# Last two value products of a granule side by side in two PSUM banks, and VectorE's squares and copies behind its partial sums

## Chip, cores, metric

The kernel runs on one core of a Trainium2 chip. The metric is the device time of one execution in microseconds (us), and the spread between runs is told with it.

## The reference

Local attention with 8 global keys, followed by a two-layer network with a squared relu:

```python
# q, k, v: (4, 8, 768, 64); window of 96 keys, 8 global keys
scores = q @ k.T / 8 + bias(slope of the head, distance);  masked outside window and globals
a = softmax(scores)
x = (a @ v).transpose(0, 2, 1, 3).reshape(3072, 512)
h = x @ w_in                       # 512 -> 2048
g = s * relu(h) ** 2 + b
return g @ w_out                   # 2048 -> 512
```

## The kernel before

The 3072 rows are worked off in 12 granules of 256 rows; three granules make one batch entry. Granule j passes through attention while TensorE also computes the first layer of granule j-1 (called m in the code) and the second layer of granule j-2 (called l). The program gives each engine its instructions in the order of its lines, so this order decides who waits. Names used below:

- S: scores of two head pairs into two score banks, then exp on ScalarE; S_mul: the mask multiply on VectorE.
- A(j, hp): value product of head pair hp, hp = 0 to 3. A_norm: reciprocal and multiply on VectorE, which writes xn.
- XT_dma: two DMA transposes xn -> xT, issued on SyncE's queue.
- P1(m, f), in steady granules r(f): eighth f of the first layer, 8 matmuls of 256 columns into a "psh" bank (there are two); relu on ScalarE empties it. Q(m, f) or "act": the square of that eighth, on VectorE or ScalarE.
- W_mm(l, n): one of seven products of a Strassen-like second layer, 8 matmuls each; W_post(l, n): its partial sum on VectorE. Granules 0 to 2 use the plain second layer P2 instead.
- KO and VO: copies of the key and value rings for the next granule.

The value product, which takes its bank by tag:

```python
def A(j, hp, tag="av", norm=True):
    av = PS[tag].tile([P, GB, 2, 65], F32, name="ps_av", tag=tag)   # "av": one bank, "psh": two
    ...  # 8 matmuls (6 in the first granule of a batch entry), 65 columns each
    if norm:
        A_norm(j, hp)
```

A steady granule (5 to 11; granules 3 and 4 are written by another function, `period`):

```python
S((0, 1))
if j > 5:
    Q(m - 1, 7)
W_mm(l, 1)
if j + 2 < NJ:
    pace(j)               # GpSimd waits for xT[j-1], then
    load_granule(j + 2)   # issues the loads of granule j+2
r(0)                      # first use of xT[j-1] = xT[m]
S_mul(j, 0)
W_post(l, 1)
W_mm(l, 2)                # uses a score bank: waits for the exp of S(0)
...
r(2)
W_sw(l, 2)
A(j, 1, norm=False)
A_norm(j, 1)
S((2, 3))
...
r(3)
W_mm(l, 6)
W_post(l, 6)
S_mul(j, 2)
r(4)
Q(m, 3)
S_mul(j, 3)
W_mm(l, 7)
A(j, 2, norm=False)
A_norm(j, 2)
W_post(l, 7)
Q(m, 4)
r(5)
A(j, 3, norm=False)
A_norm(j, 3)
XT_dma(j)
W_mm(l, 5)
W_sw(l, 4)
KO(j + 1); XB(j + 2)      # XB: DMA transposes of k and q
W_post(l, 5)
Q(m, 5)
r(6)
W_mm(l, 4)
VO(j + 1)
W_post(l, 4)
Q(m, 6)
W_mm(l, 3)
W_post(l, 3)              # reads the second score bank and so frees it
W_store(l)
r(7)
W_sw(m, 3)
```

The softmax here doesn't subtract the row's maximum and nothing guards it: scores larger than these inputs give would overflow.

Of the kernel before, what the change touches and what calls it, by code (L numbers as in the profile page):

```python
# [18 lines left out]
def kernel(  # L19
# [407 lines left out]
    def A(j, hp, tag="av", norm=True):  # L427
        b, g = bg(j)
        first = g == 0
        pt = pts.pop((j, hp))  # L430
        if j not in xn:
            xn[j] = xpool.tile([P, GB, H, D], BF16, name="xn", tag="xn", bufs=2)
        av = PS[tag].tile([P, GB, 2, 65], F32, name="ps_av", tag=tag)
        for i in range(GB):
            for hi in range(2):
                h = 2 * hp + hi
                if first:
                    ops = [(i, vaug[b % 2][:, i, h, 0:65])]
                    if i == 1:
                        ops.append((2, vaug[b % 2][:, 0, h, 0:65]))  # L440
                else:
                    ops = [
                        ((0, 3)[i], vaug[b % 2][:, g * GB + i, h, 0:65]),
                        ((1, 2)[i], vos[j][:, i, h, 0:65]),
                    ]
                for n_, (c, vv) in enumerate(ops):
                    nc.tensor.matmul(  # L447
                        av[:, i, hi, :],
                        lhsT=pt[:, hi, c * P : (c + 1) * P],
                        rhs=vv,  # L450
                        start=n_ == 0,
                        stop=n_ == len(ops) - 1,
                    )
        avs[j, hp] = av
        if norm:
            A_norm(j, hp)
            flush()
# [64 lines left out]
    def P1(j, fp, sq="dve"):  # L522
        if j not in gT:
            gT[j] = gpool.tile([P, FC, GT], BF16, name="gT", tag="gT")
        ps = ps_h.tile([P, 2, GT], F32, name="ps_1", tag="psh")
        for i in range(2):
            fc = 2 * fp + i
            for kc in range(KC):
                nc.tensor.matmul(  # L529
                    ps[:, i, :],  # L530
                    lhsT=w_in_bf[:, kc, fc * P : (fc + 1) * P],
                    rhs=xT[j][:, kc, :],
                    start=(kc == 0),
                    stop=(kc == KC - 1),
                )
        gs = gT[j][:, 2 * fp : 2 * fp + 2, :]
        flush()
        if j < W0:
            nc.scalar.activation(gs, ps[:], ACT.Relu)  # L539
        else:  # L540
            nc.scalar.activation(  # L541
                gs.rearrange("p f (r t) -> p f r t", r=2),
                ps[:].rearrange("p f (t r) -> p f r t", r=2),
                ACT.Relu,
            )
        if sq == "act":
            nc.scalar.activation(gs, gs, ACT.Square)  # L547
        elif sq == "late":
            late_sq[j, fp] = gs
        else:  # L550
            pend.append(gs)
# [3 lines left out]
    def Q(j, fp):  # L555
        gs = late_sq.pop((j, fp))
        nc.vector.tensor_tensor(gs, gs, gs, ALU.mult)  # L557
# [97 lines left out]
    def W_sw(j, n):  # L655
        t = gpool.tile([P, HF, P], BF16, name=f"sw{n}", tag=f"sw{n}", bufs=1)
        sw[j, n] = t[:]
        i0, i1, op = {
            1: lambda: (g_blk(j, 1, 0), g_blk(j, 1, 1), ALU.add),
            2: lambda: (sw[j, 1], g_blk(j, 0, 0), ALU.subtract),  # L660
            3: lambda: (g_blk(j, 0, 0), g_blk(j, 1, 0), ALU.subtract),
            4: lambda: (g_blk(j, 0, 1), sw[j, 2], ALU.subtract),
        }[n]()
        nc.vector.tensor_tensor(t[:], i0, i1, op)

    def W_mm(j, n):
        flush()
        if n == 1:
            wt[j, "a"] = ps_o.tile([P, DM], F32, name="ps_w", tag="pso")[:, 0:HC]
        elif n == 2:  # L670
            wt[j, "c"] = ps_a.tile([P, 2, DM], F32, name="ps_wa", tag="scA")[:, 0, 0:HC]
        elif n == 5:
            wt[j, "b"] = ps_b.tile([P, 2, DM], F32, name="ps_wb", tag="scB")[:, 0, 0:HC]
        elif n == 0:
            wt[j, "d"] = ps_a.tile([P, 2, DM], F32, name="ps_wd", tag="scA")[:, 0, 0:HC]
        ps, lhs, rhs, first = {
            1: lambda: ("a", g_blk(j, 0, 0), w_blk(0, 0), True),
            2: lambda: ("c", g_blk(j, 0, 1), w_blk(1, 0), True),
            6: lambda: ("a", sw[j, 2], tw[:, 1], False),
            7: lambda: ("a", sw[j, 3], tw[:, 2], False),  # L680
            5: lambda: ("b", sw[j, 1], tw[:, 0], True),
            4: lambda: ("a", g_blk(j, 1, 1), tw[:, 3], False),
            3: lambda: ("b", sw[j, 4], w_blk(1, 1), False),
            0: lambda: ("d", sw[j, 4], w_blk(1, 1), True),
        }[n]()
        for f in range(HF):
            nc.tensor.matmul(  # L687
                wt[j, ps],
                lhsT=lhs[:, f, :],
                rhs=rhs[:, f, :],  # L690
                start=first and f == 0,
                stop=f == HF - 1,
                skip_group_check=True,
            )
# [229 lines left out]
    def period(j, items, at, late=None, mid=()):  # L924
        SS(j, (0, 1))
        if j + 2 < NJ:
            pace(j)
            load_granule(j + 2)
        run(items, at[0])
        A(j, 0)  # L930
        run(items, at[1])
        A(j, 1)
        for x in mid:
            W_tw(*x)
        SS(j, (2, 3))
        run(items, at[2])
        A(j, 2)
        KO(j + 1)
        run(items, at[3])
        A(j, 3)  # L940
        if late is None:
            XT_dma(j)
        if j + 1 < NJ:
            VO(j + 1)
        if j + 2 < NJ:
            XB(j + 2)
        if late is not None:
            run(items, 1)
            late()
            XT_pe(j, "act", "psh")  # L950
        run(items, 100)
# [1 line left out]
    P2b(0)  # L953
    P2b(1)
    for f in range(4):
        P1(2, f, "act")
    period(
        3,
        [
# [6 lines left out]
            (P2, 2, 0),  # L966
            (P2, 2, 1),
            (P2, 2, 2),
            (P2_bias, 0, 0),
            (P2, 2, 3),  # L970
            (P2_bias, 0, 1),
        ],
        (3, 1, 3, 1),
# [11 lines left out]
    def steady(j):  # L985
        m, l = j - 1, j - 2
        r = lambda f: P1(m, f, "late")

        def S(hps):
            for hp in hps:  # L990
                S_mm(j, hp)
            for hp in hps:
                S_post(j, hp, mul=False)
# [5 lines that stand above are left out]
        if j + 2 < NJ:  # L999
            pace(j)  # L1000
            load_granule(j + 2)
        r(0)
        S_mul(j, 0)
        W_post(l, 1)
        W_mm(l, 2)
        W_sw(l, 1)
        S_mul(j, 1)
        r(1)
        A(j, 0, norm=False)
        W_post(l, 2)  # L1010
        A_norm(j, 0)
        r(2)
        W_sw(l, 2)
        A(j, 1, norm=False)
        A_norm(j, 1)
        S((2, 3))
        Q(m, 0)
        Q(m, 1)
        for f, *a in more(j):
            f(*a)  # L1020
        Q(m, 2)
        r(3)
        W_mm(l, 6)
        W_post(l, 6)
        S_mul(j, 2)
        r(4)
        Q(m, 3)
        S_mul(j, 3)
        W_mm(l, 7)
        A(j, 2, norm=False)  # L1030
        A_norm(j, 2)
        W_post(l, 7)
        Q(m, 4)
        r(5)
        A(j, 3, norm=False)
        A_norm(j, 3)
        XT_dma(j)
        W_mm(l, 5)
        W_sw(l, 4)
        if j + 1 < NJ:  # L1040
            KO(j + 1)
        if j + 2 < NJ:
            XB(j + 2)
        W_post(l, 5)
        Q(m, 5)
        r(6)
        W_mm(l, 4)
        if j + 1 < NJ:
            VO(j + 1)
        W_post(l, 4)  # L1050
        Q(m, 6)
        W_mm(l, 3)
        W_post(l, 3)
        W_store(l)
        r(7)
        W_sw(m, 3)

    for j in range(4, NJ):
        m, l = j - 1, j - 2
        if l < W0:  # L1060
            items = [(P1, m, 0, "act"), (P2, l, 4), (P1, m, 1), (W_tw, 2, 0, 4)]
            items += [(P2, l, 5), (P1, m, 2, "act"), (P2, l, 6), (P1, m, 3), (P1, m, 4, "act")]
            items += [(P2, l, 7), (P1, m, 5, "act"), (P1, m, 6, "act"), (W_tw, 4, 0, 4), (P1, m, 7), (W_sw, m, 3), (W_tw, 4, 4, 8)]
            items[-5:-5] = more(j)
            period(j, items, (4, 2, 2, 1), mid=((2, 4, 8),))
        else:
            steady(j)
    l, m = NJ - 2, NJ - 1
# [74 lines left out]
```

## Time and profile before

| | before |
|---|---|
| time, median of 3 runs | 213.97 us (213.65 to 214.09) |
| span of the profiled run | 211.3 us |
| TensorE busy | 96% |
| VectorE busy | 79% |
| ScalarE busy | 57% |
| granted TensorE clock | 1.00 |

The head of the page of the kernel before (busy us, share of the span, number of instructions):

```profile
span 211.3 us, 5585 instructions
PE 202.4 (96%) x2284; PEld 159.2 (75%) x2293; DVE 166.8 (79%) x400; ACT 120.8 (57%) x185; POOL 71.1 (34%) x98
```

TensorE is what the kernel is short of, but the share alone doesn't say what is left to win. The Trainium skill says so too (page "Perfetto Trace Analysis", section "Identifying the Most-Contended Engine": matmul busy time is no good measure of the distance to the limit). What helps is to read starts: a group of 8 matmuls of 256 columns takes 0.87 us from its start to the start of what follows when nothing waits. A start that comes later is a hole. (A group told with fewer matmuls than it has lacks a record, and a hole just there isn't real.)

The place of the hole, in granules 5 and 6. The timeline of TensorE before (start, duration, engine, line, operation, count; in brackets the idle time and its releaser):

```profile
79.32 1.05 PE L687 MATMUL ps_w<-w_out_bf,gT 128*128 128x256 bf16 x8
80.90 1.03 PE L529 MATMUL ps<-xT,w_in_bf 128*128 128x256 bf16 x8 [0.53 <-DMA xT<-xn]
81.77 1.04 PE L687 MATMUL ps_wa<-w_out_bf,gT 128*128 128x256 bf16 x8
...
95.37 1.05 PE L687 MATMUL ps_w<-w_out_bf,gT 128*128 128x256 bf16 x8
96.30 1.03 PE L529 MATMUL ps<-xT,w_in_bf 128*128 128x256 bf16 x8
97.17 1.04 PE L687 MATMUL ps_wa<-w_out_bf,gT 128*128 128x256 bf16 x8
```

In granule 5 the first W product starts at 79.32 and P1 could follow at 80.19; it starts at 80.90, a hole of 0.7 us, and waits for transposed x. In granule 6 the same place has 0.93 us, so hardly a hole. Granule 10 has one of 0.4 us (157.24 to 158.52).

The last two value products of granule 4, in the same view:

```profile
72.09 1.04 PE L529 MATMUL ps<-xT,w_in_bf 128*128 128x256 bf16 x8
73.47 0.20 PE L447 MATMUL ps_av<-vaug,pt 128*128 128x65 bf16 x1 [0.35 <-DVE pt L419]
...
73.73 1.03 PE L529 MATMUL ps<-xT,w_in_bf 128*128 128x256 bf16 x8
74.94 0.20 PE L447 MATMUL ps_av<-vaug,pt 128*128 128x65 bf16 x1 [0.17 <-DVE xn L465]
```

The third waits for the mask multiply (72.96 to 73.47), the fourth for the norm of the third, because both have the one "av" bank (74.60 to 74.94). And the scores of granule 7:

```profile
110.35 0.28 PE L396 MATMUL ps_s<-qT,ko 64*128 64x128 bf16 x4
110.64 0.29 PE L396 MATMUL ps_s<-qT,kT 64*128 64x128 bf16 x4
```

Four score matmuls take 0.11 to 0.12 us; the step of 0.29 us is a hole of 0.18 us, where the second score bank was still being read by the partial sum W_post(l, 3).

The waits for the weight loads of value products and of P1 (total us, times, longest), before:

```profile
PEld L447 <- DVE xn L465: 2.5, 6, 0.7
PEld L529 <- issue: 2.2, 5, 0.8
PEld L447 <- DVE pt L419: 1.3, 3, 0.6
```

### The profile page before, as it was taken

The page shows a single profiled execution, that of the slowest core. Times are in us where ns is not written, and L with a number is a line of the kernel's source. Part 1 is how long each engine was busy: PE and PEld are TensorE (multiplying, and loading weights), DVE is VectorE, ACT ScalarE, POOL GpSimd, SP SyncE. Part 2 cuts the span into 40 slices and gives each one's busy share as a digit, 9 for nine tenths or more (in the row PEclk, how much of TensorE's full clock was granted, in tenths as well). Part 3 has the DMA queues.
Part 4 walks back from the last instruction along what each step waited for, and adds up shares of the span by engine and source line. Part 5 has one row for each costly group of instructions (what it writes and reads, how often), then busy time and mean ns, then how long its engine had stood idle before and what let it go on. Part 6 is the DMA issues. An engine that isn't in the chain of part 4 may idle for free.

```text
span 211.3 us, 5585 instructions
## 1 busy us (share of the span) xinstructions
PE 202.4 (96%) x2284; PEld 159.2 (75%) x2293; DVE 166.8 (79%) x400; ACT 120.8 (57%) x185; POOL 71.1 (34%) x98
## 2 busy tenths in 40 slices
PE   7989999999999998999999999999999999999992
PEld 2556977456666677887888888888878888888882
DVE  3575658599689698987898898888898899887683
ACT  5559899445997767626536636636445546524400
POOL 8994664930181906407307209109000000000000
PEclk9999999999999999999999999999999999999999
DMA  6999999999499997998999979989965031040022
GB/s 166 192 185 195 187 201 189 180 133 152 75 96 133 235 116 105 172 177 119 145 164 113 204 83 118 200 107 107 210 86 145 36 98 54 0 149 3 0 102 99
DMA packets 103849, 27.63 MB, mean 131 GB/s; under 512 B 91408, under 2 KB 101904, under 8 KB 103824
## 3 DMA queue, kind: packets, MB, share of 16 engines
q0 software_dynamic: 70976, 13.11, 83.1%
q1 hardware_dynamic: 31792, 13.64, 31.8%
q10 hardware_dynamic: 1056, 0.52, 0.9%
q8 instruction: 18, 0.29, 0.6%
q14 instruction: 7, 0.06, 0.1%
HBM read 27.26 MB, written 6.29 MB: 159 GB/s over the span
## 4 chain that ended last, share of the span: by engine, by line
PE 79%; ACT 8%; DMA 5%; DVE 4%; issue 2%; SPq 1%; ACTq 0%
PE ps L529 34%; PE ps_w L687 14%; PE ps_wb L687 6%; PE ps L590 6%; PE ps_av L447 5%; PE ps_s L396 5%; PE ps_wa L687 4%; DMA xT<-xn 3%; ACT pt L409 3%; ACT gT L539 2%; DMA raw<-in_k_dram 2%; DVE xn L465 2%; PE ps_2s L590 2%; PE ps_s L380 1%; ACT gT L547 1%
## 5 line engine op out<-in xcount | busy, mean ns | idle before, releaser
L529 PE MATMUL ps<-xT,w_in_bf 128*128 128x256 bf16 x768 | 97.0, 273 | 1.1 <-DMA xT<-xn 0.8
L529 PEld LDWEIGHTS <-w_in_bf 128*128 128x128 bf16 x768 | 72.5, 98 | 12.9 <-issue 2.2
L541 ACT ACTIVATE gT<-ps 128x512 bf16<-128x512 f32 x72 | 43.0, 597 | 60.1 <-PE ps L529 58.5
L409 ACT ACTIVATE pt<-ps_s 128x1024 bf16<-128x1024 f32 (+1 forms) x48 | 43.1, 952 | 3.0 <-PE ps_s L396 2.9
L419 DVE TENSOR_TENSOR pt<-pt,tmpl 128x1024 bf16<-128x1024 bf16 (+1 forms) x40 | 25.8, 647 | 7.3 <-ACT pt L409 7.0
L687 PEld LDWEIGHTS <-sw 128*128 128x128 bf16 x288 | 27.7, 98 | 3.2
L557 DVE TENSOR_TENSOR gT<-gT 128x512 bf16<-128x512 bf16 x64 | 25.6, 416 | 3.2 <-ACT gT L541 3.1
L112 POOL DMA_DIRECT2D vaug<-in_v_dram x24 | 21.6, 919 | 3.8 <-DMA w_out_bf<-in_moe_w_out_dram 1.8
L687 PEld LDWEIGHTS <-gT 128*128 128x128 bf16 x216 | 20.6, 98 | 3.0
L465 DVE TENSOR_TENSOR xn<-ps_av,rc 128x256 bf16<-128x256 f32 x48 | 20.4, 424 | 1.9 <-DVE rc L464 0.3
L447 PEld LDWEIGHTS <-pt 128*128 128x128 bf16 x352 | 14.9, 98 | 7.5 <-DVE xn L465 2.5
L590 PE MATMUL ps<-w_out_bf,gT 128*128 128x512 bf16 x74 | 18.8, 379 | 0.5 <-issue 0.3
L447 PE MATMUL ps_av<-vaug,pt 128*128 128x65 bf16 x224 | 17.5, 194 | 1.6 <-DVE rc L464 0.6
L687 PE MATMUL ps_w<-tw,sw 128*128 128x256 bf16 x144 | 18.7, 273 | 0.0
L697 DVE SCALAR_TENSOR_TENSOR u<-ps_w,s_bc,bvec 128x256 f32<-128x256 f32 x27 | 12.9, 479 | 6.1 <-PE ps_w L687 6.1
L104 POOL DMA_DIRECT2D qnat<-in_q_dram x18 | 16.0, 904 | 3.2 <-DMA w_out_bf<-in_moe_w_out_dram 1.8
L104 POOL DMA_DIRECT2D knat<-in_k_dram x18 | 15.8, 887 | 3.1 <-issue 2.7
L539 ACT ACTIVATE gT<-ps 128x512 bf16<-128x512 f32 x24 | 14.2, 597 | 4.4 <-PE ps L529 4.3
L126 POOL COPY pdum<-xT 1x1 bf16<-1x1 bf16 x5 | 0.9, 187 | 45.1 <-DMA xT<-xn 45.1
L464 DVE RECIPROCAL rc<-ps_av 128x4 f32<-128x4 f32 x48 | 8.6, 179 | 8.5 <-PE ps_av L447 8.4
L590 PEld LDWEIGHTS <-gT 128*128 128x128 bf16 x96 | 8.6, 98 | 8.2
L396 PE MATMUL ps_s<-qT,kT 64*128 64x128 bf16 x224 | 12.7, 219 | 0.3
(94 smaller groups left out, 241.6 us busy)
## 6 DMA issues: line engine op xcount, KB each, us to landing
out_dram<-o_pr SPq DMA_DIRECT2D x8, 512.0 KB, 4.2
vaug<-in_v_dram POOLq DMA_DIRECT2D x24, 128.0 KB, 7.3
knat<-in_k_dram POOLq DMA_DIRECT2D x22, 128.0 KB, 5.0
qnat<-in_q_dram POOLq DMA_DIRECT2D x22, 128.0 KB, 6.5
w_in_bf<-in_moe_w_in_dram POOLq DMA_DIRECT2D x8, 256.0 KB, 8.3
w_out_bf<-in_moe_w_out_dram POOLq DMA_DIRECT2D x4, 512.0 KB, 9.9
out_dram<-o_pr SPq DMA_DIRECT2D x7, 256.0 KB, 4.0
raw<-in_q_dram ACTq DMA_DIRECT2D x2, 256.0 KB, 4.8
```

What stands on the lines that cost most here:

```text
L104: nc.gpsimd.dma_start(t[:, i, :, :], src[b, :, sb * P : (sb + 1) * P, :].rearrange("h p d -> p h d"))
L112: nc.gpsimd.dma_start(vaug[b % 2][:, sb, :, 0:D], v[b, :, sb * P : (sb + 1) * P, :].rearrange("h p d -> p h d"),)
L396: nc.tensor.matmul(ps[:, hi, oc * P : (oc + 1) * P], lhsT=kt[r, :], rhs=qT[j][r, hp, i * P : (i + 1) * P], start=not biased, stop=not bias ...
L409: nc.scalar.activation(pt[:, :, 0:n], ps[:, :, 0:n], ACT.Exp, scale=QSCALE)
L419: nc.vector.tensor_tensor(pt[:, :, 0:n], pt[:, :, 0:n], m, ALU.mult)
L447: nc.tensor.matmul(av[:, i, hi, :], lhsT=pt[:, hi, c * P : (c + 1) * P], rhs=vv, start=n_ == 0, stop=n_ == len(ops) - 1,)
L465: nc.vector.tensor_tensor(xn[j][:, :, 2 * hp : 2 * hp + 2, :], av[:, :, :, 0:D], rc[:].to_broadcast((P, GB, 2, D)), ALU.mult,)
L529: nc.tensor.matmul(ps[:, i, :], lhsT=w_in_bf[:, kc, fc * P : (fc + 1) * P], rhs=xT[j][:, kc, :], start=(kc == 0), stop=(kc == KC - 1),)
L541: nc.scalar.activation(gs.rearrange("p f (r t) -> p f r t", r=2), ps[:].rearrange("p f (t r) -> p f r t", r=2), ACT.Relu,)
L557: nc.vector.tensor_tensor(gs, gs, gs, ALU.mult)
L590: nc.tensor.matmul(po[j, tb], lhsT=gT[j][:, fc, tb * P : (tb + 1) * P], rhs=w_out_bf[:, fc, :], start=(fc == 0), stop=(fc == FC - 1),)
L687: nc.tensor.matmul(wt[j, ps], lhsT=lhs[:, f, :], rhs=rhs[:, f, :], start=first and f == 0, stop=f == HF - 1, skip_group_check=True,)
```

## The change

The fourth value product moves in front of r(5), next to the third, and takes a "psh" bank; so xn is complete one P1 sooner and x is transposed sooner. The second value product takes a "psh" bank too. VectorE does the partial sums first, then the ring copies and squares. In granule 5 the first P1 goes behind the second W product. In granules 3 and 4 some squares change engine and the order is adapted. The core of the diff:

```diff
     # period (granules 3 and 4)
-        A(j, 1)
+        A(j, 1, "psh")
...
-        A(j, 3)
+        A(j, 3, "psh")
...
-        P1(2, f, "act")
+        P1(2, f, "act" if f % 2 else "late")
+    Q(2, 0)
+    Q(2, 2)
...
     # granule 4
-            period(j, items, (4, 2, 2, 1), mid=((2, 4, 8),))
+            period(j, items, (4, 2, 3, 0), mid=((2, 4, 8),))
...  # P1(3, 3) squared on ScalarE, P1(3, 6) on VectorE
     # steady granules
-        r(0)
+        if j > 5:
+            r(0)
         S_mul(j, 0)
         W_post(l, 1)
         W_mm(l, 2)
+        if j == 5:
+            r(0)
...
-        A(j, 1, norm=False)
+        A(j, 1, "psh", norm=False)
...
         r(4)
-        Q(m, 3)
         S_mul(j, 3)
         W_mm(l, 7)
         A(j, 2, norm=False)
+        A(j, 3, "psh", norm=False)
         A_norm(j, 2)
-        W_post(l, 7)
-        Q(m, 4)
-        r(5)
-        A(j, 3, norm=False)
         A_norm(j, 3)
         XT_dma(j)
+        W_post(l, 7)
+        r(5)
         W_mm(l, 5)
         W_sw(l, 4)
+        W_post(l, 5)
         KO(j + 1); XB(j + 2)
-        W_post(l, 5)
-        Q(m, 5)
         r(6)
+        Q(m, 3)
+        Q(m, 4)
         W_mm(l, 4)
+        W_post(l, 4)
         VO(j + 1)
-        W_post(l, 4)
-        Q(m, 6)
         W_mm(l, 3)
         W_post(l, 3)
         W_store(l)
+        Q(m, 5)
+        Q(m, 6)
```

More of the change, by code (lines that the diff above doesn't have):

```diff
@@ L968 @@
             (P2, 2, 2),
+            (P2, 2, 3),
             (P2_bias, 0, 0),
-            (P2, 2, 3),
             (P2_bias, 0, 1),
@@ L1061 @@
             items = [(P1, m, 0, "act"), (P2, l, 4), (P1, m, 1), (W_tw, 2, 0, 4)]
-            items += [(P2, l, 5), (P1, m, 2, "act"), (P2, l, 6), (P1, m, 3), (P1, m, 4, "act")]
-            items += [(P2, l, 7), (P1, m, 5, "act"), (P1, m, 6, "act"), (W_tw, 4, 0, 4), (P1, m, 7), (W_sw, m, 3), (W_tw, 4, 4, 8)]
+            items += [(P2, l, 5), (P1, m, 2, "act"), (P2, l, 6), (P1, m, 3, "act"), (P1, m, 4, "act")]
+            items += [(P2, l, 7), (P1, m, 5, "act"), (P1, m, 6), (W_tw, 4, 0, 4), (P1, m, 7), (W_sw, m, 3), (flush,), (W_tw, 4, 4, 8)]
             items[-5:-5] = more(j)
-            period(j, items, (4, 2, 2, 1), mid=((2, 4, 8),))
+            period(j, items, (4, 2, 3, 0), mid=((2, 4, 8),))
         else:
```

## The prediction

> **What bounds the kernel now.** TensorE. In the profile's first part it is busy 96% of the 211.3 us span, at a granted clock of 1.00, and the chain of waits that ended last is 79% TensorE. The Trainium skill (page "Perfetto Trace Analysis", section "Identifying the Most-Contended Engine") warns that matmul busy time overstates how near TensorE is to its limit, so I read start-to-start times. In the timeline a group of 8 matmuls (256 columns) starts 0.87 us after the one before, all through the steady granules 6 to 11: one such period takes 15.4 to 15.7 us, of which 8 first-layer and 7 second-layer groups are 15 x 0.87 = 13.1, scores about 1.0, value products about 1.0. Almost nothing is to be won there.
>
> **What can be won: holes in TensorE's timeline (start of the next group less 0.87 us after the last).**
> - Granule 10: first P1 waits for transposed x: 158.11 to 158.52, 0.4 us.
> - Granule 5: the same, 80.19 to 80.90, 0.7 us.
> - Granule 4: third value product waits for the mask multiply (72.96 to 73.47, 0.5 us), fourth for the norm of the third, sharing its bank (74.60 to 74.94, 0.3 us).
> - Granule 3 with P1(2): ScalarE does relu (0.58) plus square (0.63) for each 0.87 us of matmul from 49.4 to 55.2: about 0.2 us at the fourth P1, 0.2 at A(3,1), 0.1 at P2(2,4).
> Sum 2.4 us.
>
> **What the change does.** No operation is added or removed; squares change engine: two of P1(2) go from ScalarE (0.63) to VectorE (0.42), one of P1(3) each way. The fourth value product goes before r(5), so xn is ready about 0.7 us earlier (one P1 of 0.87, less the norm of 0.6 that must queue on VectorE); the transposing DMA takes 4.5 to 5.2 us from issue to first use, so the 0.4 us of granule 10 should go. For granule 5 the first P1 is put behind W_mm 2, which fills the 0.7 us hole, less a possible 0.1 to 0.3 wait for the exp that frees that bank. In granule 4 P1(4) moves before A2: the 0.5 wait goes, A3 then waits about 0.2 for the second mask multiply. In granule 3, less ScalarE work removes about 0.3.
>
> Gain about 1.7 us. Costs: the second value product now takes a turn of the two P1 banks, so P1 r(3) waits for the relu of r(2): that ends at 116.40, r(3) starts at 116.52, so 0 to 0.1 us per period. VectorE, 89% busy in steady periods, gets the same work in another order; delayed squares (5, 6, 7) may come just late for W_mm 2 once or twice. I take 0.3 us off.
>
> **Prediction:** 213.97 - 1.4 = 212.5 us; 8 in 10: 211.1 to 213.9. Faster by over 2%: 0.02; within 2%: 0.97; slower: 0.01.
>
> **What would show it.** The wait of P1 for transposed x (0.8 us in TensorE's wait view) vanishes; the xT transposes are issued about 0.7 us earlier after the fourth value product; the wait of value products for xn (2.5 us, weight-load view) falls by 0.3 to 0.8; ScalarE busy falls by about 1.3 us, VectorE rises by 0.8; from 50 to 81 us the schedule shortens by about 1.3 us; each steady period stays at 15.4 to 15.7 us.
>
> **What would make it wrong.** New TensorE waits each steady period: r(3) on relu, A3 on the second mask multiply (within 0.1 us of the need), or W_mm 2 on late squares: 0.2 us in each of seven periods would eat the gain. Or the earlier transposes land no sooner.

## The result

| | before | after |
|---|---|---|
| time, median of 4 runs | 214.01 us (213.65 to 214.09) | 211.87 us (211.07 to 211.90) |
| ratio | | 0.989 (95%: 0.987 to 0.992) |
| span of the profiled run | 211.3 us | 209.3 us |

So 2.1 us, 1%: clear of noise, and under the 2% that would count as faster. A ratio here is the mean time of one kernel's fast runs over that of the other's in the same rounds, so it isn't quite the ratio of the medians quoted. The head of the page after:

```profile
span 209.3 us, 5603 instructions
PE 201.1 (96%) x2293; PEld 160.8 (77%) x2293; DVE 167.0 (80%) x402; ACT 119.6 (57%) x183; POOL 74.5 (36%) x98
```

Shares tell nothing here. Granules 5 and 6 in TensorE's timeline after:

```profile
78.20 1.05 PE L687 MATMUL ps_w<-w_out_bf,gT 128*128 128x256 bf16 x8
79.31 1.03 PE L687 MATMUL ps_wa<-w_out_bf,gT 128*128 128x256 bf16 x8
80.18 1.91 PE L529 MATMUL ps<-xT,w_in_bf 128*128 128x256 bf16 x16
...
93.71 1.05 PE L687 MATMUL ps_w<-w_out_bf,gT 128*128 128x256 bf16 x8
95.78 1.03 PE L529 MATMUL ps<-xT,w_in_bf 128*128 128x256 bf16 x8 [1.02 <-DMA xT<-xn]
96.65 1.04 PE L687 MATMUL ps_wa<-w_out_bf,gT 128*128 128x256 bf16 x8
```

In granule 5 the hole of 0.7 us is down to 0.24 us (79.31 instead of 79.07). But in granule 6 there is a new one: P1 could start at 94.58 and starts at 95.78, 1.2 us later, waiting for the transposed x of granule 5. That x was issued sooner, as meant. SyncE's queue before and after (start of issue first):

```profile
91.46 3.49 SPq L508 DMA_TRANSPOSE xT<-xn  x2
```

```profile
89.11 3.41 SPq L508 DMA_TRANSPOSE xT<-xn  x2
```

It was issued 2.35 us sooner and was in use 0.52 us sooner (P1 at 95.78 instead of 96.30). The time from issue to landing of its two transposes, each counted from its own issue, in the view of this tile, before and after:

```profile
DMA to landing us min/median/max: 3.5/3.9/4.3
```

```profile
DMA to landing us min/median/max: 5.3/5.7/6.0
```

From the first issue to the last landing the pair took 4.70 us before and 6.54 after. Where one number is given for a pair below, it is counted in this way.

The last value products of granule 4 and the scores of granule 7 after (the other lines of the third and fourth product left out):

```profile
71.51 1.91 PE L529 MATMUL ps<-xT,w_in_bf 128*128 128x256 bf16 x16
73.26 0.19 PE L447 MATMUL ps_av<-vaug,pt 128*128 128x65 bf16 x1
...
73.81 0.20 PE L447 MATMUL ps_av<-vaug,pt 128*128 128x65 bf16 x1
...
109.61 0.28 PE L396 MATMUL ps_s<-qT,ko 64*128 64x128 bf16 x4
109.72 0.28 PE L396 MATMUL ps_s<-qT,kT 64*128 64x128 bf16 x4
```

The third product no longer waits. The fourth follows the third in 0.55 us where 0.25 would do, since the second mask multiply is just late. The hole in the scores of granule 7 is gone. The weight-load waits after:

```profile
PEld L529 <- DMA xT<-xn: 1.3, 1, 1.3
PEld L447 <- DVE xn L465: 1.0, 2, 0.7
PEld L447 <- DVE pt L419: 0.6, 2, 0.3
```

**A ledger of the lead.** The start of a granule's scores marks its place on TensorE. I count it from the first weight load of P1(2,0), where the edited part begins; in front of that the program is the same, but it takes 49.1 to 49.7 us in the profiles, and that alone would blur the reading. Numbers worked out from starts in the traces:

| us from P1(2,0) to | before | after | lead |
|---|---|---|---|
| scores of granule 3 | 4.04 | 3.80 | 0.24 |
| granule 4 | 15.90 | 15.38 | 0.52 |
| granule 5 | 29.57 | 28.44 | 1.13 |
| granule 6 | 45.73 | 44.06 | 1.67 |
| granule 7 | 61.03 | 60.28 | 0.75 |
| granule 8 | 76.69 | 75.67 | 1.02 |
| granule 9 | 92.29 | 91.07 | 1.22 |
| granule 10 | 107.29 | 106.11 | 1.18 |
| granule 11 | 123.35 | 121.56 | 1.79 |
| end | 162.10 | 160.10 | 2.00 |

The lead grows to 1.67 us by granule 6, falls by 0.92 us there, and grows again. Two questions remain: what each part of the change is worth, and why the transposed x of granule 5 lands so late after its issue.

### The profile page after: what moved, and what is told of

The parts are those of the page before. It is cut to its first block, busy times and chain, and to the rows that moved or that the text cites. A ratio compares the mean times of both kernels' runs of the same rounds, so it can differ in the third digit from the quotient of the medians.

```text
span 209.3 us, 5603 instructions
## 1 busy us (share of the span) xinstructions
PE 201.1 (96%) x2293; PEld 160.8 (77%) x2293; DVE 167.0 (80%) x402; ACT 119.6 (57%) x183; POOL 74.5 (36%) x98
## 4 chain that ended last, share of the span: by engine, by line
PE 77%; ACT 10%; DVE 5%; DMA 4%; issue 2%; SPq 0%; ACTq 0%
PE ps L529 34%; PE ps_w L687 14%; PE ps_wb L687 6%; PE ps L590 5%; PE ps_av L447 4%; PE ps_s L396 4%; PE ps_wa L687 4%; ACT pt L409 3%; ACT gT L539 3%; DMA xT<-xn 3%; DMA raw<-in_k_dram 2%; PE ps_2s L590 2%; PE ps_s L380 1%; DVE xn L465 1%; ACT gT L547 1%
## 5 line engine op out<-in xcount | busy, mean ns | idle before, releaser
L419 DVE TENSOR_TENSOR pt<-pt,tmpl 128x1024 bf16<-128x1024 bf16 (+1 forms) x40 | 25.2, 647 | 3.4 <-ACT pt L409 2.9
L557 DVE TENSOR_TENSOR gT<-gT 128x512 bf16<-128x512 bf16 x66 | 25.1, 415 | 1.8 <-ACT gT L541 1.6
L590 PE MATMUL ps<-w_out_bf,gT 128*128 128x512 bf16 x80 | 19.7, 379 | 0.0
L126 POOL COPY pdum<-xT 1x1 bf16<-1x1 bf16 x5 | 4.5, 898 | 42.0 <-DMA xT<-xn 42.0
L447 PEld LDWEIGHTS <-pt 128*128 128x128 bf16 x352 | 15.4, 98 | 3.9 <-DVE xn L465 1.0
L447 PE MATMUL ps_av<-vaug,pt 128*128 128x65 bf16 x224 | 16.4, 193 | 1.0 <-DVE rc L464 0.6
```

The lines of the kernel that those rows point to most:

```text
L419: nc.vector.tensor_tensor(pt[:, :, 0:n], pt[:, :, 0:n], m, ALU.mult)
L447: nc.tensor.matmul(av[:, i, hi, :], lhsT=pt[:, hi, c * P : (c + 1) * P], rhs=vv, start=n_ == 0, stop=n_ == len(ops) - 1,)
L557: nc.vector.tensor_tensor(gs, gs, gs, ALU.mult)
L590: nc.tensor.matmul(po[j, tb], lhsT=gT[j][:, fc, tb * P : (tb + 1) * P], rhs=w_out_bf[:, fc, :], start=(fc == 0), stop=(fc == FC - 1),)
```

## The experiments

Each row of runs that was timed is given with its ratio to the kernel before of the same rounds.

### Parts of the change alone

**r0_only.** The kernel before, with one edit:

```diff
-        r(0)
+        if j > 5:
+            r(0)
...
         W_mm(l, 2)
+        if j == 5:
+            r(0)
```

> The kernel before, with one thing of the change: in granule 5 the first P1 is put behind the second W product. Theory A (leads add up): the 0.7 us hole in front of P1 is filled, less about 0.25 us wait for the bank of the second W product, so 213.5 us, 0.5 less than before. Theory B (an xT landing is tied to the other DMA traffic, not only to its issue): the granule 6 hole in front of P1 opens by up to 0.5 us instead, and the total is 213.8 to 214.0.

Measured: 213.42 us, ratio 0.9991 (0.9975 to 1.0007): no difference shown. Neither theory foresaw the reason. TensorE's timeline of granule 5:

```profile
79.36 1.05 PE L687 MATMUL ps_w<-w_out_bf,gT 128*128 128x256 bf16 x8
...
81.02 1.03 PE L687 MATMUL ps_wa<-w_out_bf,gT 128*128 128x256 bf16 x8 [0.62 <-ACT pt L409]
```

The hole of 0.7 us stayed at the same place (0.79 us) and only changed its name: the second W product needs a score bank, and ScalarE's exp that frees it begins late, at 79.96, behind relus and squares of granule 3. With the other edits of the change that exp is in time, and 0.24 us of wait is left.

**periods_only.** The kernel before with all edits of granules 3 and 4 (the squares of P1(2), the "psh" tags in `period`, the list of granule 4, and the P2 order).

> The kernel before, with the edits of granules 3 and 4 alone. In the profile after, TensorE was ahead by 1.1 us at the scores of granule 5. Theory A: 1.1 us stays to the end, 212.9 us. Theory B: the xT of granule 4 lands only 0.85 us sooner (as in the profile after), so the hole in front of the first P1 of granule 5 grows from 0.7 to about 1.0 us, and 213.2 us or more remain.

Measured: 212.18 us, ratio 0.9936 (0.9917 to 0.9956), 1.4 us by the means. In its profile the lead at the scores of granule 5 is 1.13 us, the same as in the kernel after. Then it loses 0.7 us at once: the hole in front of the first P1 of granule 5 has grown from 0.71 to 1.41 us, because its transposed x landed 4.84 us after issue instead of 4.39. So theory B was right about the place. The same happens again in granule 10: its transposes are issued 0.82 us sooner than before and land 0.26 us sooner, its hole is 0.98 us instead of 0.41, and of the lead about 0.2 us is left at the end. This hole differs from profile to profile: with the same order of granules 5 to 11 it is 0.41 us in before, but 0.87 in r0_only and 0.89 in squares_only. The profiled run of periods_only was the slowest of the six (212.89 us), and the median is 0.7 us better than it.

**steady_only.** The kernel before with the edits of granules 5 to 11, without the moved r(0).

> The kernel before, with the edits of the steady granules 5 to 11 alone, without the move of the first P1 in granule 5. The hole of granule 10 (0.4 us) and small waits for a value product's bank (0.3 us in granule 6, 0.2 at the scores of granule 7) go: 212.8 to 213.2 us. Theory A (issue sooner means landing sooner) says no hole for xT in granule 6. Theory B says that the xT of granule 5 is issued about 0.7 us sooner and lands hardly sooner, 4.5 to 5.5 us after issue instead of 3.5 to 4.3, but as TensorE is not ahead here, no hole opens in granule 6 either. Tells apart by the time to landing.

Measured: 212.51 us, ratio 0.9936 (0.9918 to 0.9955), a little better than expected. Its transposes of granule 5 were issued 0.46 us sooner than before and landed 0.65 us sooner. Counted as in the expectation, each from its own issue, they took 2.5 and 3.9 us (before: 3.5 and 4.3), less than theory B expected; for the pair it is 4.51 us instead of 4.70. Granule 6 had no hole. So here theory A fits. But the hole of granule 10, which was to go, is 0.74 us in this profile: its transposes took 6.0 us.

The three parts give 0.2, 1.4 and 1.3 us by the means, 2.9 together. The whole gives 1.7 to 2.3 us in two sets of rounds. So about 0.6 to 1.2 us of the parts' gain is not additive (each figure has an interval of 0.3 to 0.6 us to either side). That is about the size of the new hole of granule 6; that it is the cause is likely but not shown by these sums.

**squares_only.** The kernel before, with only the squares:

```diff
     for f in range(4):
-        P1(2, f, "act")
+        P1(2, f, "act" if f % 2 else "late")
+    Q(2, 0)
+    Q(2, 2)
```

> The kernel before, with only two squares of P1(2) moved from ScalarE to VectorE. In the profiles the kernel after is ahead by 0.24 us at the scores of granule 3 and by 0.52 us at those of granule 4. Theory: these come from the squares alone, so both stand in the profile within 0.15 us, and nothing is gained in granule 4 (lead at the scores of granule 5 under 0.7). Total 213.2 to 213.6 us. Rival (they come from the value products' second bank in granule 3): no lead at the scores of granule 3.

Measured: 212.85 us, ratio 0.9959 (0.9937 to 0.9981), 0.9 us by the means and more than expected. The profile has leads of 0.24 us at granule 3 and 0.65 at granule 4, and 0.71 at granule 5. The squares make the whole lead of granule 3, then; the full change gives 0.13 us back by granule 4 (0.52), where P1(2, 6) has to wait 0.22 us for a relu (0.66 us from the first score to it, against 0.44 in squares_only), as A(3, 1) has taken a turn of its two banks. (The run one_bank below, without that turn, has 0.64 us there.) The 0.35 us wait of the third value product is still in this profile, and granule 4 adds only 0.06 us to the lead here, against 0.61 in the full change: that is the new order of granule 4 together with the second bank, for one_bank, which has this order and one bank, adds only 0.03 us there. The lead doesn't last in this profile, the slowest of its six: in granule 10, with its hole of 0.89 us, it falls from 0.84 to 0.37 us, and 0.07 are left at the end.

**sums_first.** The kernel before, with only VectorE's order changed in the steady granules:

```diff
-        Q(m, 3)
...
-        Q(m, 4)
...
         W_sw(l, 4)
+        W_post(l, 5)
         KO(j + 1); XB(j + 2)
-        W_post(l, 5)
-        Q(m, 5)
         r(6)
+        Q(m, 3)
+        Q(m, 4)
         W_mm(l, 4)
+        W_post(l, 4)
         VO(j + 1)
-        W_post(l, 4)
-        Q(m, 6)
         W_mm(l, 3)
         W_post(l, 3)
         W_store(l)
+        Q(m, 5)
+        Q(m, 6)
```

> The kernel before, with only the VectorE order of the steady granules changed: squares 3 to 6 and the ring copies behind the partial sums; value products stay where they were, in one bank. Theory: the partial sum that frees the second bank of the scores comes sooner, so the hole in the middle of the scores (0.2 us in granules 7, 8, 10, 11 of the kernel before) goes: 213.0 to 213.2 us, 0.6 less than before. Rival (all of the steady gain comes from the value products back to back): 213.7 us, as before.

Measured: 213.03 us, ratio 0.9960 (0.9929 to 0.9991). The hole in the scores is gone; granule 7 in TensorE's timeline:

```profile
110.34 0.28 PE L396 MATMUL ps_s<-qT,ko 64*128 64x128 bf16 x4
110.45 0.29 PE L396 MATMUL ps_s<-qT,kT 64*128 64x128 bf16 x4
```

From the scores of granule 7 to those of granule 8 the kernel before takes 15.66 us, this one 15.48, steady_only 15.39 and the kernel after 15.39. From 8 to 9: 15.60, 15.48, 15.39 and 15.40. So more than half of what an ordinary steady granule gains comes from the order of VectorE alone; 0.08 to 0.09 us more come with the value products side by side.

### The banks

**one_bank.** The kernel after, order kept, all value products in the "av" bank:

```diff
-        A(j, 1, "psh")
+        A(j, 1)
...
-        A(j, 3, "psh")
+        A(j, 3)
...
-        A(j, 1, "psh", norm=False)
+        A(j, 1, norm=False)
...
-        A(j, 3, "psh", norm=False)
         A_norm(j, 2)
+        A(j, 3, norm=False)
```

> The kernel after, order kept, but all value products in the one bank that they had before. If the second bank is what lets the last two stand back to back, the fourth value product waits in each of granules 4 to 11 for reciprocal and norm of the third, 0.7 to 0.9 us each: 217 to 219 us, with the wait of value products for xn up by 5 to 7 us. The rival (order alone gives the gain, the bank does not matter) says 212 us.

Measured: 216.67 us, ratio 1.0143 (1.0125 to 1.0161): slower than before by 3.0 us. The waits of the value products' weight loads:

```profile
PEld L447 <- DVE xn L465: 8.2, 11, 0.9
```

From 1.0 to 8.2 us; in each of granules 4 to 11 the fourth product starts 0.89 or 0.90 us late. This is just what the Trainium skill has in mind (page "Perfetto Trace Analysis", section "Matmuls": independent groups should rotate through different PSUM banks, so that the emptying of one overlaps the next group), and this trace gives it a number. The bank for the fourth product is what makes the new order possible.

**a1_one_bank.** The kernel after, with only the second value product of the steady granules back in "av":

```diff
-        A(j, 1, "psh", norm=False)
+        A(j, 1, norm=False)
```

> The kernel after, with the second value product of the steady granules back in the bank of the first. The other bank for it costs in the profile after 0.22 us in granules 6 and 9, where P1(3) waits for a relu, and saves the wait for the norm of the first (0.28 us in granule 6 before, 0.05 in the others). Theory: the two cancel, 211.7 to 212.1 us. Rival (that bank is worth something in every granule): 212.5 us or more.

Measured: 211.99 us, ratio 0.991 (0.989 to 0.993), against 211.91 us and 0.992 of the kernel after in the same rounds. No difference shown: with the bank, the fourth P1 waits 0.13 us for a relu in granules 6 and 9 (0.57 us from the first score to it, against 0.44 in this run; the 0.22 us of the expectation took too short a step as undisturbed); without it, the second value product waits less than 0.15 us in each granule. The runs show no gain from that part of the change.

### Why the transposed x comes late

The loads of granule 7 (six of 128 KB) are issued in granule 5, and so are three stores of 256 KB of the plain second layer. In the landing records of the trace after, the last load lands at 93.81 us and the last store at 93.73; the transposes issued at 89.11 land at 95.64. The Trainium skill says that DMAs issued from SyncE, ScalarE and GpSimd all run on the same 16 DMA engines and interleave (page "Trainium Kernel Development and Optimization", section "Key Constraints"). Theory: the transposes share the engines with what is in flight, and an earlier issue only means a longer wait. Two runs take some of the traffic away.

**loads5_late.** The kernel after; in granule 5 the loads wait for the landing of that granule's own transposed x:

```diff
-        if j + 2 < NJ:
+        if j + 2 < NJ and j != 5:
             pace(j)
             load_granule(j + 2)
...
         XT_dma(j)
+        if j == 5:
+            nc.gpsimd.tensor_copy(pdum[:], xT[j][0:1, KC - 1, GT - 1 : GT])
+            load_granule(j + 2)
```

> The kernel after, but the loads of granule 7 are issued only when the xT of granule 5 has landed. Theory (that transposing DMA shares the DMA engines with loads and stores in flight): it lands about 4 us after its issue instead of 6.5, and the wait of P1 for xT in granule 6 (1.2 us) is gone. Rival (it is slow by itself, or because of the stores alone): 5.5 us or more, and a wait of 0.5 us or more stays. The total says little, as the loads may then hold up later transposes.

**no_stores.** The kernel after, without three of the stores; its output is wrong, as rows are left unwritten:

```diff
+        if j < 2 or tb == 0:          # in P2_out
             nc.sync.dma_start(out[t0 : t0 + P, :], o_sb)
...
+        if j == 0:                    # in P2_bias
             nc.sync.dma_start(out[t0 : t0 + P, :], o_sb)
```

> The kernel after, three stores of 256 KB of granules 1 and 2 left out (wrong output on purpose). If the stores that are still in flight in granule 5 are what delays its xT, it lands 4 to 4.5 us after issue instead of 6.5 and the wait of 1.2 us in granule 6 is gone, 210.7 to 211.0 us. If the loads alone do it, 6 us and 211.8 us.

Measured: time from issue to landing of the two transposes of granule 5, in the view of the tile xT, first loads5_late, then no_stores:

```profile
DMA to landing us min/median/max: 2.4/2.7/3.1
```

```profile
DMA to landing us min/median/max: 2.5/3.2/3.9
```

Against 5.3/5.7/6.0 in the kernel after. For the pair it is 4.3 and 4.5 us against 6.5, as both expectations had it. In both the wait of P1 for x in granule 6 is gone. In no_stores (the W product at 93.69, P1 0.88 us later):

```profile
93.69 1.05 PE L689 MATMUL ps_w<-w_out_bf,gT 128*128 128x256 bf16 x8
94.57 1.04 PE L529 MATMUL ps<-xT,w_in_bf 128*128 128x256 bf16 x8
```

no_stores took 210.26 us (ratio 0.984), 1.6 us less than the 211.87 of the kernel after, though not in the same rounds; the hole was 1.2. loads5_late took 217.1 us (ratio 1.0165), because the loads then met the next granule's transposes: those landed 9.1 us after issue, and granule 7 lost 4.7 us in two large holes. The total of that run was not the point, and its mean granted clock (0.982) was the lowest: after the first large hole the clock reads 0.52 from 112 to 115 us, 0.50 to 117 and 0.52 to 119, and a group of 8 matmuls took 1.7 us instead of 0.87. So the landing depends on the traffic in flight: with either the loads or the stores gone, it is 2 us faster. The rival that the transposes are slow by themselves falls: in granule 10 of the kernel after, where no loads are left, the same two take 3.7 us from first issue to last landing, against 6.5 in granule 5.

How the traffic delays them stays open: both runs fit the shared engines of the skill, but neither shows the sharing itself, and two rivals were not tested. One is the order in SyncE's own queue, which the stores share with the transposes: in the DMA packet records of the trace after, the stores' packets (2048 bytes) run to 92.94 us, and the first packet of the transposes (256 bytes) comes at 91.59, 2.48 us after the issue; in before, no_stores and loads5_late it comes 1.2 us after. Loads alone did no harm in granule 6 of the kernel after: three of them landed during the flight of its transposes, which took 3.74 us. The other rival is the fetching of instructions. Over granules 4 to 11 of all 14 profiles, 55 pairs of transposes had no packet of the instruction queues (q8 and q14, 16 and 8 KB) in flight beside them, and 49 of these took 3.7 to 3.8 us; each of the 32 pairs with a q8 packet and no q14 packet took 4.1 to 6.0. In granule 5 of the kernel after there is one of each. But traffic alone can do it too: the 9.1 us of loads5_late had no such packet.

### A version that beats both

**after_again.** The kernel after once more, for the same rounds.

> The kernel after, unchanged, so that the next runs have it on the same chip and in the same rounds: 211.1 to 211.9 us as before.

Measured: 211.91 us (211.20 to 213.06), ratio 0.9919 (0.9891 to 0.9946). In this profile the hole of granule 6 is 1.66 us, the transposes landing 7.0 us after issue, and granule 10 still has a hole of 0.28 us.

**r0_5_6.** The kernel after, with the second W product drawn into the hole of granule 6 as well:

```diff
-        if j > 5:
+        if j > 6:
             r(0)
...
-        if j == 5:
+        if j <= 6:
             r(0)
```

> The kernel after, with the first P1 put behind the second W product in granule 6 too. In the profile after, the first P1 of granule 6 waits 1.2 us for transposed x, and the second W product (0.87 us) could run in that hole: the exp that frees its bank ends 0.1 us after the first W product there. Theory: the hole shrinks to about 0.3 us, 211.0 us, 0.8 less than the kernel after. Rival (the time is lost again at the next xT that is late, in granule 10): 211.4 to 211.9, with a hole of 0.4 to 0.9 us there.

Measured: 210.73 us (210.56 to 210.94), ratio 0.9857 (0.9828 to 0.9886). TensorE in granule 6:

```profile
93.71 1.05 PE L687 MATMUL ps_w<-w_out_bf,gT 128*128 128x256 bf16 x8
94.72 1.03 PE L687 MATMUL ps_wa<-w_out_bf,gT 128*128 128x256 bf16 x8
96.01 1.92 PE L529 MATMUL ps<-xT,w_in_bf 128*128 128x256 bf16 x16 [0.25 <-DMA xT<-xn]
```

The hole is filled but for 0.42 us (and 0.14 in front of the W product), and the lead stays to the end: nothing is lost in granule 10 (hole 0.06 us), against the rival. In the profiles of periods_only and squares_only above a lead was lost there, so the rival is refuted for this run alone. This is also the direct proof that the hole cost time. The like edit of granule 5 gained nothing in r0_only, so it pays only where the exp is not late.

**w6_first.** r0_5_6 and the third W product in front of the fourth P1:

```diff
-        r(3)
         W_mm(l, 6)
+        r(3)
         W_post(l, 6)
```

> The kernel after, with the first P1 put behind the second W product in granules 5 and 6, and the third W product put before the fourth P1 in all steady granules, so that the relu of the third P1 has 0.87 us more before its bank is needed. Theory: the two holes of 0.22 us (granules 6 and 9) go, 210.3 us against 210.7 without that; 1.2 to 1.6 us less than the kernel after. Rival: the third W product then waits for its own sum on VectorE, and it is 210.7 or more.

Measured: 210.58 us (210.17 to 212.59), ratio 0.9863 (0.9825 to 0.9901), 1.3 us under after_again by the medians. The two holes of 0.13 us (called 0.22 in the expectation) are gone from its profile. Its hole of granule 6 is larger than in r0_5_6 (0.74 us and 0.14), as its transposes took 7.2 us. But against r0_5_6 the intervals overlap and the two were never in the same rounds, so whether this last step gains anything stays open. What is settled is that r0_5_6 and w6_first both beat the kernel before by 1.4%, and w6_first beats the kernel after in the same rounds, by means of 210.87 against 212.01 us (1.1 us; 95% interval from these twelve times 0.1 to 2.2, so only just clear of the noise).

## Why the prediction was right, and where it wasn't

Predicted were 212.5 us (211.1 to 213.9) and no difference over 2%; measured were 211.87 us. So it was right, with 1.4 us predicted as the gain and 2.1 measured. The sum, term by term, with the profiles after and before:

- **Granule 3, ScalarE's squares: 0.3 us predicted, 0.5 measured, 0.65 by the squares alone.** The mechanism was right. I had missed that the exp behind the squares also delayed the mask multiply that the first value product waits for (0.24 us).
- **Granule 4, third and fourth value products: about 0.6 predicted (0.8 of holes, 0.2 left), 0.6 measured** (lead from 0.52 to 1.13 us). One hole of 0.31 us is left, at the second mask multiply as foreseen.
- **Granule 5, r(0) behind the second W product: 0.4 to 0.6 predicted, 0.5 measured** (0.71 to 0.24 us). r0_only shows that this came only together with the edits of granules 3 and 4, which I had not said.
- **Granule 10: 0.4 predicted, 0.34 in the first profile** (0.07 us left), and less in another (0.28 left). This term is uncertain, as the hole with the old order of the steady granules was 0.41 to 0.98 us in four profiles (before, r0_only, periods_only, squares_only).
- **"Each steady period stays at 15.4 to 15.7 us": wrong in size.** 15.66 and 15.60 became 15.39 and 15.40 (granules 7 and 8; granule 9 gained nothing, 15.00 and 15.04). I read the periods as full, because the idle time of TensorE was 0.0 in the windows. My own sum (13.1 + 1.0 + 1.0 = 15.1 us) already left 0.3 to 0.6 us of each period without a place. The hole of 0.18 us in the scores and the small losses at each value product lie in the time that the profile counts as busy. sums_first shows that VectorE's order alone gives the larger part. Over granules 7 to 11 this gave about 0.9 us (the lead from 0.75 to 2.00, less 0.34 of granule 10).
- **"The wait of P1 for transposed x vanishes": wrong.** It went from 0.8 to 1.0 us in TensorE's wait view, from granules 5 and 10 to granule 6, where it made a hole of 1.2 us. The issue was indeed earlier: in granule 7 it stands 10.34 us after the first P1 instead of 11.10, about 0.7 as predicted, though the sum given for it (0.87 less 0.6) doesn't give 0.7. What failed is the step from issue to landing, for which I took 4.5 to 5.2 us as fixed. It was 6.5 to 7.0 us in granule 5 of the kernel after, and 3.7 to 3.8 in its granules 6, 8, 10 and 11. I had named this as what would make the prediction wrong ("or the earlier transposes land no sooner"), without giving it a size.
- **Costs: 0.3 predicted.** P1(3) waits 0.13 us in granules 6 and 9 and P1(2, 6) 0.22 us in granule 3, instead of 0 to 0.1 in each granule. No W product waited for a late square.

The two large errors, 0.9 us too little in the steady granules and 1.2 us too little cost in granule 6, nearly cancel. That the total fell into the range owes something to this.

For the other signs: ScalarE's busy time fell by 1.2 us (1.3 predicted); VectorE's rose by 0.2 (0.8 predicted), as other groups there, such as the mask multiplies, were shorter. The wait of value products for xn fell from 2.5 to 1.0 us, more than the 0.3 to 0.8 predicted.

Left open: why the transposes of granule 9, used in granule 10, take 5.1 to 6.0 us from first issue to last landing in all profiles, even in no_stores (a q8 instruction packet runs beside them in each of these profiles and beside none of those of granules 10 and 11, which take 3.7 to 3.8; whether it is the cause was not tested); and what makes the difference of up to 0.6 us between profiles in front of the edited part.

## What to carry to other kernels

When an engine is shown as busy all the time, measure from start to start against the undisturbed step, because waits of 0.1 to 0.3 us hide in the busy time, and a repeated one adds up. When you move work sooner, ask whether what follows it, a DMA above all, can also end sooner; if it can't, as in granule 6 here, the time is waited for later. And fill a hole with work whose own inputs are certainly there: the same move of one line gained nothing in one surrounding (r0_only) and about a microsecond in another (r0_5_6: 210.73 us, against 211.87 and 211.91 of the kernel after in other rounds).

## What the Trainium skill lacked or had wrong

- TensorE: Matmul & The Clock Gate, section "Back-to-back issue gap", gives two figures for 512 columns: a sustained 131 ns in a stream with weight loads, and 518 cycles (about 216 ns) for the isolated gap. Here the plain second layer, a stream of weight loads and matmuls of 512 columns, runs at 216 ns each (8 matmuls from 47.69 to 49.42 us in the trace after), so the second figure holds for the stream. For 256 columns its 262 cycles agree: 0.109 us.
- DMA: Bandwidth & Descriptors: its section "DMA Transpose (X-bar)" tells the constraints; how long a small transpose takes beside loads and stores in flight I did not find there. Here the same pair of transposes in SBUF took 3.7 us from first issue to last landing where no loads were left, and 6.5 to 7.0 us with three loads of 128 KB and three stores of 256 KB still under way at its issue.
- Perfetto Trace Analysis, section "Identifying the Most-Contended Engine", is right that matmul busy time misleads; what it does not give for TensorE is the way that worked here, steps from start to start (the page advises them for GpSimd). Idle time of TensorE in the windows from 102 to 148 us was 0.02 us before, while a steady granule could still be cut by 0.2 to 0.27 us.
